# A fused linear attention and feed-forward kernel: the opening plan written anew, with batch 0's keys and values in the row layout of the later batches and w_out loaded in halves

## The chip, the cores and the metric

The kernel runs on one core of one Trainium2 chip. The metric is the device time of one execution in microseconds (us). The kernel before takes 250.07 us, the median of 3 runs (249.78 to 250.11).

## The reference

`q`, `k`, `v` have the shape 8 batches, 8 heads, 576 positions, 64 values, in fp32. The weights `w1`, `w2` are 512x1024, `w3` is 1024x1024, `w_out` 1024x512. Attention is linear, with ReLU features that are scaled by the cosine and the sine of the position:

```python
q_p = phi(q, cos_w, sin_w)          # [relu(x)*cos, relu(x)*sin], 128 features
k_p = phi(k, cos_w, sin_w)
kv = np.einsum('bhsf,bhsd->bhfd', k_p, v)
z = np.sum(k_p, axis=2)
num = np.einsum('bhsf,bhfd->bhsd', q_p, kv)
den = np.einsum('bhsf,bhf->bhs', q_p, z)[..., None] + 1e-06
attn = num / den                    # then heads are joined: x is 4608 x 512
out = ((x @ w1) * (x @ w2)) @ w3 @ w_out
```

## The kernel before

Attention works batch by batch, in five chunks of positions (four of 128 rows, one of 64). The feed-forward part works on nine tiles of 512 tokens. `w3 @ w_out` is multiplied once on the chip into `w34`, so that a tile needs only the products with `w1`, `w2` and `w34`.

The order of all work is a hand-written list, `PLAN`, whose steps are issued one after the other. Every engine runs its own instructions strictly in the order in which the steps issue them. The steps that matter here, with a batch `b` and a chunk `c`:

- `l b t h`, `lg`, `lt`: half `h` of tensor `t` of batch `b` is loaded by a DMA that POOL issues (`lg` and `lt` first wait for a result that is named in the code). `l0 ...`: the same for parts of batch 0. `w12 i c n`: `n` column blocks of 128 of `w1` (i=0) or `w2` (i=1). `w3 p`, `wo p`: pieces of `w3` and `w_out`. All these convert fp32 to bf16 on the way. Batch 0's keys alone are loaded by SP, in fp32.
- `k b c`, `q b c`: the features of keys and queries. VectorE (DVE) makes the cosine half (L502), ScalarE (ACT) the sine half (L505); a third number `n` gives the first `n` heads of the sine half to ScalarE and the rest to VectorE (L508).
- `v b c E`: the values are copied beside a column of ones, on engine E (V, A or G).
- `kv b` (L548), `kv0` (L746): the matmuls of keys and values. `kvs0`: their copies out of PSUM.
- `qt`, `qh`: a chunk of query features is transposed on TensorE (PE, L566 and L559) and copied out by the engine named. `qd` does the same by a DMA transpose that SP issues.
- `n b c` (L580): the numerators and denominators. `d b c` (L589 to L591): the division. `xt` (PE, L618) or `xd` (DMA): the transposes of the result into the tile `xT`.
- `t3 j`: VectorE transposes block `j` of 128 rows of `w3` (L464). `w j l n` (L480): `n` of the eight matmuls that make block `j` of `w34`; ScalarE copies it out (L483). Block `j` needs the rows of `w3` of that block in all four partition groups, and all of `w_out`.
- `f t`: the next step of tile `t`. A tile's steps are the products with `w1` and `w2` (L662), in two halves of 256 tokens for the first four column blocks of the tiles 0 and 1 and then one column block at a time; ScalarE copies the `w1` product (L686, L700) and VectorE multiplies it with the `w2` product (L688, L705). Tile 0 takes 16 steps of these. Then come 8 steps of output matmuls (L710). PSUM tiles of these products come from one pool of four buffers, used in turn.
- `idle n`: `n` matmuls on zeros, whose results nobody reads.

POOL has eight lanes for its loads: a load is issued when the load that was issued eight before it has landed. Both kernels have this through the framework. Before the first `f 0`, the plan is one long line; afterwards each line begins with one step of PE's main work.

In the layout of the batches 0 and 7 ("whole"), partition p holds positions 4p to 4p+3 of the first 512, and the last 64 positions are a chunk of their own, loaded by a separate DMA in pieces of 64 values. In the row layout of the batches 1 to 6, partitions 0 to 63 hold five positions each of the first 320, and partitions 64 to 127 four each of the last 256.

Of the kernel before, what the change touches and what calls it, by code (L numbers as in the profile page):

```python
# [10 lines left out]
FP32 = mybir.dt.float32  # L11
BF16 = mybir.dt.bfloat16
# [4 lines left out]
P = 128  # L17
H, S, D = 8, 576, 64
# [8 lines left out]
l0 q02; k 0 4; k 0 0; idle 10; l0 v4; v 0 0 A; w12 1 0 2; k 0 2; l0 q22; lg 1 q 0; l0 q4; lg 1 q 1; w12 0 0 2; w12 1 4 2; w12 0 2 2; v 0 4 V; v 0 1 V; v 0 2 A; k 0 3; w12 1 6 2; idle 3; w12 1 2 2; q 0 1; w12 0 4 2; w3 3; k 0 1; w3 1; qt 0 1 V; q 0 0 4; w12 0 6 2; wo 1; qc 0 3; v 0 3 A; wo 0; kv0; q 0 2; kvs0 1 A; kvs0 0 A; w3 0; wo 3; w3 2; qh 0 0 V; wo 2; qs 0 3; n 0 1; qt 0 2 A; w3 4; d 0 1; w3 5; qt 0 3 A; q 0 4; n0; w3 6; n 0 2; d 0 0; idle 3; d 0 2; xt 0 1 V; open; w3 7; xt 0 0 A; q 1 2; q 1 0; lg 1 k 0; n 0 3; qt 0 4 V; lg 1 k 1; lg 1 v 0; lt 1 v 1; xt 0 2 A; q 1 3; q 1 1; l 2 k 0  # L27
f 0
f 0; d 0 3
f 0; l 2 v 0  # L30
f 0; xt 0 3 V; qt 1 2 V; n 0 4; d 0 4
f 0
f 0; clear 1
f 0
f 0
f 0; xt 0 4 V
f 0
f 0; qt 1 0 V; lg 2 q 0; q 1 4; qt 1 3 A
f 0; qt 1 1 V
f 0  # L40
f 0; l 2 k 1; t3 0
f 0
f 0; t3 1; qt 1 4 A
w 0 0 4
w 0 4 4; l 2 q 1
w 1 0 4
w 1 4 4; t3 2; t3 3; t3 4
w 2 0 4
w 2 4 4; l 2 v 1; v 1 4 G
w 3 0 4; v 1 3 G; t3 5; v 1 1 G  # L50
w 3 4 4
w 4 0 4; k 1 2; l 3 q 0; t3 6
w 4 4 4; k 1 1; t3 7; k 1 4
w 5 0 4
w 5 4 4; k 1 0
w 6 0 4; v 1 2 V
w 6 4 4; v 1 0 V; k 1 3
w 7 0 4; kv 1
w 7 4 4; v 2 3 G; n 1 4; v 2 0 G
f 0; d 1 4  # L60
f 0; n 1 0; xd 1 4; d 1 0
f 0; q 2 1; v 2 4 G; lt 3 v 0; q 2 0
f 0; n 1 1; d 1 1; k 2 2
f 0; q 2 3
f 0; lg 3 q 1; v 2 1 G; l 3 v 1; q 2 4; k 2 0
f 0; n 1 2; d 1 2
f 0; xt 1 1 V; lt 3 k 0
f 1; k 2 3; xd 1 0; n 1 3; d 1 3; xt 1 2 V
f 1; qd 2 1
f 1; v 2 2 V  # L70
f 1; k 2 4; k 2 1
f 1
f 1; kv 2; l 3 k 1
f 1; qd 2 0; q 2 2; qd 2 2
# [237 lines left out]
def kernel(  # L312
# [53 lines left out]

    def load(b, name, part=None):
# [22 lines left out]
    def load_first(eng, t, src, c0=0, n=4):  # L390
        rows = src[0, :, 0:512, :].rearrange("h (p j) d -> p h j d", j=4)
        eng.dma_start(out=t[:, :, c0:c0 + n, :].rearrange("p h j d -> p h (j d)"),  # L392
                      in_=rows[:, :, c0:c0 + n, :].rearrange("p h j d -> p h (j d)"))

    def load_first4(eng, t, src):
        eng.dma_start(out=t[0:64, :, 4, :], in_=src[0, :, 512:S, :].rearrange("h p d -> p h d"))  # L396

    def load_w3(piece):

        half, a = divmod(piece, 4)  # L400
        nc.gpsimd.dma_start(out=w3b[ts(a, 32), ts(half, 4), :].rearrange("p g (c j) -> p (g c) j", c=4),
                            in_=moe_w3[ts(half, 512), ts(a, 256)].rearrange("(r i) j -> i r j", i=32))

    def load_wout(a):

        nc.gpsimd.dma_start(out=woutb[ts(a, 32), :, :],
                            in_=moe_w_out[ts(a, 256), :].rearrange("(l j) m -> j l m", j=32))

    def load_w12(c0, n):
        nc.gpsimd.dma_start(out=w1b[:, :, ds(c0, n)], in_=w1v[:, :, ds(c0, n)])  # L410
        nc.gpsimd.dma_start(out=w2b[:, :, ds(c0, n)], in_=w2v[:, :, ds(c0, n)])
# [7 lines left out]
    def load_first_parts(what):  # L419

        name, n = what[0], int(what[1])
        t, src = raw[0, name], {"v": v, "q": q}[name]
        if n == 4:
            load_first4(nc.gpsimd, t, src)
        else:
            load_first(nc.gpsimd, t, src, n, int(what[2]))
# [9 lines left out]
    def clear_rows(i):  # L436

        if i < NVA:
            nc.vector.memset(va_bufs[i][:, :, :, D:D + 1], 1.0)
            nc.vector.memset(va_bufs[i][64:128, 4, :, 0:D], 0.0)  # L440
        for fp in kp_bufs[i:i + 1] + qp_bufs[i:i + 1]:
            nc.vector.memset(fp[64:128, 4, :, :], 0.0)

    clear_rows(0)
# [13 lines left out]
    make_identity(nc, identb[:])  # L458


    def w3_tr(jp):

        w3T = sm.tile([P, 8, 128], BF16, name="w3T", bufs=NT3)
        nc.vector.transpose(out=w3T[:].rearrange("p l (c i) -> p l c i", c=4),  # L464
                            in_=w3b[:, jp, :].rearrange("p (c l j) -> p l c j", c=4, l=8))
        w3Ts[jp] = w3T

    def w3_dma(jp):
        w3Ts[jp] = sm.tile([P, 8, 128], BF16, name="w3T", bufs=NT3)
        nc.sync.dma_start_transpose(out=w3Ts[jp][:], in_=w3b[:, jp, :])  # L470
        transposed[0] = w3Ts[jp][:, 0, 0:1]
# [25 lines left out]
    def features(b, dst, src, c, n=H, cos=True, sin=True):  # L497

        R = ROWS[c]
        at = NCH + c if b in WHOLE else c  # L500
# [10 lines left out]
    def prep_k(b, c, n=H, **kw):  # L511
        features(b, att_of(b)["kp"], raw[b, "k"], c, n, **kw)

    def prep_q(b, c, n=H, **kw):
        features(b, att_of(b)["qp"], raw[b, "q"], c, n, **kw)

    def prep_v(b, c, copy=None):
        R = ROWS[c]
        (copy or nc.gpsimd.tensor_copy)(out=att_of(b)["va"][:R, c, :, 0:D], in_=raw[b, "v"][:R, :, c, :])  # L519
# [35 lines left out]
    def q_tr_halves(b, c, on):  # L555
        for half in range(2):
            pst = ps_tr.tile([P, 8, 128], BF16, name="pst")
            for i in range(4):
                nc.tensor.transpose(pst[:, i, :], att[b]["qp"][:, c, 4 * half + i, :], identb[:])  # L559
            on(out=att[b]["qpT"][:, ts(half, 4), ds(columns_of(b, c), 128)], in_=pst[:, 0:4, :])  # L560
# [178 lines left out]
    def kv_first():  # L739

        kp, va = att_of(0)["kp"], att_of(0)["va"]
        att[0]["kvs"] = sm.tile([P, H, D + 1], BF16, name="kvs", bufs=2)
        halves = att[0]["halves"] = (kva[:, :], pnum()[:, 0, :])
        for c in range(NCH):
            for h in range(H):
                nc.tensor.matmul(halves[h // 4][:, ds((h % 4) * 65, 65)], lhsT=kp[:, c, h, :],  # L746
                                 rhs=va[:, c, h, 0:D + 1], start=(c == 0 and h % 4 == 0),
                                 stop=(c == NCH - 1 and h % 4 == 3))
# [39 lines left out]
    def store_behind_transposes():  # L788
# [7 lines left out]
        "l": load, "lg": gated, "lt": behind_transposes, "l0": load_first_parts, "gx": behind_first_x,  # L796
# [44 lines left out]
```

## Time and profile before

| | us |
|---|---|
| median of 3 runs | 250.07 |
| the profiled execution, whole | 249.93 |
| its span, first to last instruction | 248.0 |
| what lies around the span | 1.93 |
| PE busy | 238.7 |
| VectorE busy | 141.4 |
| ScalarE busy | 126.7 |
| POOL busy | 85.0 |

PE is busy for 96% of the span. Its granted clock shows as full speed in all 40 slices. The profile's chain of work that ended last goes back through PE for 87% of the span and through DMA for 8%. Times in the text are counted from the start of the span. The landing of a load is the start of its issue on POOL plus the time to landing that the view of DMA issues gives. The sizes of that view are those in which the data land, in KB of 1024 bytes.

### The profile page before, as it was taken

To read this page: it belongs to the slowest core of one execution; us is meant where nothing else is said; L and a number is where in the kernel's file an instruction comes from. 1 tells how busy PE (TensorE), PEld (TensorE's weight loads), DVE (VectorE), ACT (ScalarE), POOL (GpSimd) and SP (SyncE) were. 2 spreads that over 40 slices of the span, in tenths; PEclk is the share of its full clock that TensorE was granted. 3 is DMA by queue.
4 is the path that set the end of the run, shared out by engine and by line. 5 is a ranking of instruction groups with operands and counts; after the bars stand their busy time and mean duration, and the time that the engine had idled before them with its cause. 6 is when DMAs were issued, how large, how long until landed. Compare 5 with 4: busy or idle time off the path is not lost.

```text
span 248.0 us, 4883 instructions
## 1 busy us (share of the span) xinstructions
PE 238.7 (96%) x1827; PEld 129.8 (52%) x1855; DVE 141.4 (57%) x342; ACT 126.7 (51%) x217; POOL 85.0 (34%) x162
## 2 busy tenths in 40 slices
PE   8969999999999999999999999999999999999994
PEld 3468754455974644445554545455444644444443
DVE  6498668768758545828685462577546607512420
ACT  2689243658566642765467334767643332323332
POOL 7664354534602042305310506207000100397800
PEclk9999999999999999999999999999999999999999
DMA  7999999999996989999999999999876431389933
GB/s 193 181 193 194 200 200 197 198 199 173 170 181 99 166 139 173 148 202 131 151 145 123 165 158 121 202 164 176 183 98 121 98 69 21 70 268 341 293 132 127
DMA packets 87223, 40.69 MB, mean 164 GB/s; under 512 B 51744, under 2 KB 84768, under 8 KB 87200
## 3 DMA queue, kind: packets, MB, share of 16 engines
q0 software_dynamic: 40144, 27.20, 69.6%
q1 hardware_dynamic: 47056, 13.18, 33.5%
q8 instruction: 14, 0.23, 0.4%
q14 instruction: 9, 0.07, 0.1%
HBM read 38.80 MB, written 9.44 MB: 194 GB/s over the span
## 4 chain that ended last, share of the span: by engine, by line
PE 87%; DMA 8%; POOL 2%; issue 1%; DVE 1%; ACT 0%; POOLq 0%; DVEq 0%
PE ffnps L662 49%; PE ffnps L710 24%; PE ffnps L480 5%; DMA w2b<-in_moe_w_dram 4%; PE pnum L580 4%; DMA qs<-in_q_dram 4%; PE pnum L548 4%; PE pst L566 1%; PE ffnps L727 1%; POOL vs L392 0%; POOL qs L392 0%; POOL w2b L770 0%; POOL vs L396 0%; PE pst L618 0%; DVE abT L705 0%
## 5 line engine op out<-in xcount | busy, mean ns | idle before, releaser
L705 DVE TENSOR_TENSOR abT<-asb,ffnps 128x512 bf16<-128x512 bf16 x64 | 43.7, 685 | 59.6 <-PE ffnps L662 56.7
L662 PE MATMUL ffnps<-xT,w2b 128*128 128x512 bf16 (+2 forms) x347 | 75.3, 340 | 0.9 <-DMA w2b<-in_moe_w_dram 0.3
L662 PE MATMUL ffnps<-xT,w1b 128*128 128x512 bf16 (+2 forms) x341 | 74.6, 339 | 0.5
L700 ACT CAST asb<-ffnps 128x512 bf16<-128x512 f32 x64 | 37.4, 584 | 53.7 <-PE ffnps L662 42.8
L710 PE MATMUL ffnps<-w34b,abT 128*128 128x512 bf16 x271 | 63.8, 379 | 0.5
L662 PEld LDWEIGHTS <-w2b 128*128 128x128 bf16 x352 | 31.5, 98 | 28.6 <-issue 0.5
L662 PEld LDWEIGHTS <-w1b 128*128 128x128 bf16 x352 | 31.7, 98 | 28.0
L710 PEld LDWEIGHTS <-abT 128*128 128x128 bf16 x280 | 26.1, 98 | 28.3
L505 ACT ACTIVATE kp<-kf,sinv 128x512 bf16<-128x512 bf16 (+3 forms) x40 | 28.0, 718 | 7.1 <-DMA kf<-in_k_dram 7.1
L505 ACT ACTIVATE qp<-qs,sinv 128x512 bf16<-128x512 bf16 (+2 forms) x40 | 28.0, 714 | 4.0 <-DMA qs<-in_q_dram 4.0
L591 DVE TENSOR_TENSOR xblk<-pnum,den 128x512 bf16<-128x512 f32 (+1 forms) x39 | 26.9, 691 | 2.5 <-DMA xT<-xblk 1.3
L417 POOL COPY seen<-asb 128x1 bf16<-128x1 bf16 x13 | 2.5, 194 | 54.6 <-ACT asb L700 54.6
L580 PEld LDWEIGHTS <-qpT 128*128 128x128 bf16 x320 | 15.3, 98 | 9.8 <-issue 0.9
L502 DVE TENSOR_SCALAR kp<-kf,cosv 128x512 bf16<-128x512 bf16 (+3 forms) x40 | 15.4, 404 | 7.3 <-DMA kf<-in_k_dram 7.2
L716 ACT COPY early<-ffnps 128x512 f32<-128x512 f32 x19 | 11.0, 581 | 15.8 <-PE ffnps L710 15.7
L580 PE MATMUL pnum<-kvs,qpT 128*128 128x65 bf16 x312 | 16.4, 194 | 1.4 <-DVE xblk L591 0.5
L716 ACT COPY osb<-ffnps 128x512 f32<-128x512 f32 x16 | 9.3, 584 | 14.8 <-PE ffnps L710 13.4
L519 POOL COPY va<-vs 128x512 bf16<-128x512 bf16 (+1 forms) x17 | 10.7, 648 | 17.5 <-DMA vs<-in_v_dram 17.5
L502 DVE TENSOR_SCALAR qp<-qs,cosv 128x512 bf16<-128x512 bf16 (+1 forms) x40 | 14.8, 389 | 1.9 <-DMA qs<-in_q_dram 1.9
L480 PE MATMUL ffnps<-early,w3T 128*128 128x512 bf16 x62 | 13.9, 379 | 0.1
L417 POOL COPY seen<-xT 128x1 bf16<-128x1 bf16 x8 | 1.6, 196 | 34.4 <-DMA xT<-xblk 34.4
L453 PE MATMUL unread<-zeros 128*128 128x512 bf16 x42 | 11.6, 441 | 1.2 <-DVE zeros L434 1.2
(86 smaller groups left out, 197.6 us busy)
## 6 DMA issues: line engine op xcount, KB each, us to landing
out_dram<-osb POOLq DMA_DIRECT2D x10, 256.0 KB, 4.5
qs<-in_q_dram POOLq DMA_DIRECT2D x8, 256.0 KB, 8.5
early<-in_moe_w_dram POOLq DMA_DIRECT2D x8, 256.0 KB, 10.3
qs<-in_q_dram POOLq DMA_DIRECT2D x6, 320.0 KB, 8.3
kf<-in_k_dram POOLq DMA_DIRECT2D x6, 320.0 KB, 8.0
vs<-in_v_dram POOLq DMA_DIRECT2D x6, 320.0 KB, 7.5
kf<-in_k_dram POOLq DMA_DIRECT2D x6, 256.0 KB, 6.8
vs<-in_v_dram POOLq DMA_DIRECT2D x6, 256.0 KB, 7.7
```

Of the source, the lines that this page charges most:

```text
L453: nc.tensor.matmul(unread[:, :], lhsT=zeros[:, 0:128], rhs=zeros[:], start=True, stop=True)
L480: nc.tensor.matmul(acc[:, :], lhsT=w3T[:, lc, :], rhs=woutb[:, lc, :], start=(lc == 0), stop=(lc == 7))
L502: nc.vector.tensor_scalar(out=dst[:R, c, :, 0:D], in0=src[:R, :, c, :], scalar1=0.0, scalar2=cosv[:R, at:at + 1], op0=ALU.max, op1=ALU.mult)
L505: nc.scalar.activation(out=dst[:R, c, 0:n, D:F], in_=src[:R, 0:n, c, :], func=ACTF.Relu, scale=sinv[:R, at:at + 1], bias=0.0)
L519: (copy or nc.gpsimd.tensor_copy)(out=att_of(b)["va"][:R, c, :, 0:D], in_=raw[b, "v"][:R, :, c, :])
L580: nc.tensor.matmul(nt[:, h // 4, ds((h % 4) * 65, 65)], lhsT=qpT[:, h, ds(at, 128)], rhs=kvs[:, h, :], start=True, stop=True)
L591: nc.vector.tensor_tensor(out=xblk[rows], in0=n4[:, :, :, 0:D], in1=den[rows].unsqueeze(3).to_broadcast([R, 2, 4, D]), op=ALU.mult)
L662: nc.tensor.matmul(out, lhsT=w[:, kc, ts(jc, 128)], rhs=x[:, kc, tok], start=(kc == 0), stop=(kc == 3))
L700: nc.scalar.copy(out=asb[:], in_=aT[:, :])
L705: nc.vector.tensor_mul(out=abT[:, jc, :], in0=asb[:], in1=bT[:, :])
L710: nc.tensor.matmul(ops[:, :], lhsT=abT[:, jc, ts(ms, 128)], rhs=w34b[:, jc, :], start=(jc == 0), stop=(jc == 7))
L716: nc.scalar.copy(out=osb[:, ms % 2, :], in_=ops[:, :])
```

## The change

The opening line of `PLAN` and the lines up to the second third of tile 1 are replaced. The functions that load batch 0, `w3` and `w_out` take other pieces.

- Keys and values of batch 0 are loaded in the row layout: one DMA for the partitions 0 to 63 and one for 64 to 127. Queries of batch 0 stay in the whole layout.
- `w3` comes in 16 pieces of 128 KB (two row blocks of one partition group) instead of 8 of 256 KB. `w_out` comes in 8 halves of 128 KB instead of 4 pieces of 256 KB.
- Batch 1's queries are loaded behind most of `w3` instead of ahead of `w1`. The features and transposes of batch 1's queries lie among the `w` steps or behind them, instead of among the products of tile 0.
- `kv0` goes chunk by chunk. A chunk whose values have not been copied is multiplied as 64 columns straight from the loaded values and one column from a new constant of ones (16 matmuls instead of 8).
- The first steps of `f 0` start after two chunks of batch 0; `kv 1` lies after `w 7`, not in the middle of it; steps of `f 1` are mixed with the last steps of `f 0`.
- The chunks `x 1 4`, `1 0` and `1 2` are transposed on PE and `1 1` and `1 3` by DMA. Before, `1 1` and `1 2` went through PE and `1 4`, `1 0` and `1 3` through DMA.

```diff
-l0 q02; k 0 4; k 0 0; idle 10; l0 v4; v 0 0 A; w12 1 0 2; k 0 2; l0 q22; lg 1 q 0; l0 q4; lg 1 q 1; w12 0 0 2; w12 1 4 2; w12 0 2 2; v 0 4 V; v 0 1 V; v 0 2 A; k 0 3; w12 1 6 2; idle 3; w12 1 2 2; q 0 1; w12 0 4 2; w3 3; k 0 1; w3 1; qt 0 1 V; q 0 0 4; w12 0 6 2; wo 1; qc 0 3; v 0 3 A; wo 0; kv0; q 0 2; kvs0 1 A; kvs0 0 A; w3 0; wo 3; w3 2; qh 0 0 V; wo 2; qs 0 3; n 0 1; qt 0 2 A; w3 4; d 0 1; w3 5; qt 0 3 A; q 0 4; n0; w3 6; n 0 2; d 0 0; idle 3; d 0 2; xt 0 1 V; open; w3 7; xt 0 0 A; q 1 2; q 1 0; lg 1 k 0; n 0 3; qt 0 4 V; lg 1 k 1; lg 1 v 0; lt 1 v 1; xt 0 2 A; q 1 3; q 1 1; l 2 k 0
+q0 0 2; k 0 0 4; idle 1; k 0 2; q0 4 1; q0 2 2; k 0 1; w12 1 2 2; w12 1 0 2; v 0 3 A; v 0 4 V; idle 1; idle 1; w12 0 0 2; w12 0 4 2; v 0 2 V; w12 0 2 2; k 0 3; k 0 4; idle 2; w12 0 6 2; idle 1; kv0 2 0; kv0 0 1; w12 1 6 2; idle 1; wo 3 0 4; w12 1 4 2; q 0 0 4; kv0 1 1; kv0 3 1; qh 0 0 A V; idle 3; q 0 1 4; kv0 4 2; kvs0 0 A; kvs0 1 V; qt 0 1 A; n0; idle 1; idle 2; d 0 0; idle 2; wo 0 4 4; n 0 1; w3 2 0 2; idle 1; q 0 2; wo 1 0 4; w3 3 2 2; xt 0 0 A; wo 1 4 4; qt 0 2 A; d 0 1; idle 1; idle 2; wo 0 0 4; q 0 3; wo 2 0 4; xt 0 1 V; w3 3 0 2; w3 0 0 2; open; wo 3 4 4; w3 1 0 2; w3 2 2 2; wo 2 4 4; w3 1 2 2; w3 2 4 2; w3 0 2 2; w3 3 4 2; l 1 q 0; w3 1 4 2; w3 0 4 2; q 0 4; l 1 q 1
+f 0; w3 1 6 2; w3 2 6 2; w3 3 6 2; w3 0 6 2; n 0 2; l 1 k 0; d 0 2
+f 0; l 1 k 1; qt 0 3 V
+f 0; l 1 v 0; l 1 v 1; xt 0 2 V; n 0 3
...
+f 0; xt 0 4 V; t3 0
 f 0
+f 0; lg 2 q 0; t3 1
 f 0
+f 0; t3 2; l 2 v 0
 f 0
+f 0
 w 0 0 4
+w 0 4 4; t3 3
 w 1 0 4
+w 1 4 4
 w 2 0 4
+w 2 4 4; clear 1; t3 4; q 1 0
+w 3 0 4
+w 3 4 4; l 2 k 1; q 1 4 2; l 2 q 1; v 1 4 G; t3 5
+w 4 0 4; q 1 2; q 1 1; t3 6
+w 4 4 4; qt 1 0 A; q 1 3 2; l 2 v 1
+w 5 0 4; qt 1 4 A
+w 5 4 4; v 1 1 G; t3 7
+w 6 0 4; k 1 4; v 1 3 G; k 1 2; k 1 1 4; k 1 0 4; qt 1 1 V; k 1 3 4
+w 6 4 4; l 3 q 0; v 2 4 G
+w 7 0 4; qt 1 3 A; v 1 0 V; v 1 2 V
+w 7 4 4; kv 1
+f 0; n 1 4
+f 0; d 1 4; qt 1 2 V; n 1 0; d 1 0
+f 0; xt 1 4 V
+f 0; n 1 1; lt 3 v 0; d 1 1; q 2 1
+f 0; xt 1 0 V; v 2 3 G; l 3 v 1; k 2 0
+f 0; q 2 3; v 2 2 G; n 1 2; v 2 1 G; lg 3 q 1; d 1 2
+f 1
+f 1; q 2 4; q 2 0; k 2 2; v 2 0 G; xd 1 1
+f 0; n 1 3; lt 3 k 0; d 1 3
+f 1; qd 2 1; k 2 3 2
+f 0; v 3 3 G
+f 1; q 2 2; xt 1 2 V; k 2 4; second; k 2 1
...
+    def load_rows(eng, t, rows, half):
+        j, span = (5, slice(0, 320)) if half == 0 else (4, slice(320, S))
+        eng.dma_start(out=t[ts(half, 64), :, 0:j, :].rearrange("p h j d -> p h (j d)"),
+                      in_=rows[:, span, :].rearrange("h (p j) d -> p h (j d)", j=j))
...
+    def load_w3(a, g0, n):
+        nc.gpsimd.dma_start(out=w3b[ts(a, 32), ds(g0, n), :].rearrange("p g (c j) -> p (g c) j", c=4),
+                            in_=moe_w3[ds(128 * g0, 128 * n), ts(a, 256)].rearrange("(r i) j -> i r j", i=32))
+    def load_wout(a, l0=0, n=8):
+        rows = moe_w_out[ts(a, 256), :].rearrange("(l j) m -> j l m", j=32)
+        nc.gpsimd.dma_start(out=woutb[ts(a, 32), ds(l0, n), :], in_=rows[:, ds(l0, n), :])
...
+    for eng, t, src in ((nc.sync, k0, k), (nc.gpsimd, raw[0, "v"], v)):
+        load_rows(eng, t, src[0], 0)
+        load_rows(eng, t, src[0], 1)
...
+            if c in copied:
+                nc.tensor.matmul(out, lhsT=kp[:, c, h, :], rhs=va[:, c, h, 0:D + 1],
+                                 start=(first and h % 4 == 0), stop=(last and h % 4 == 3))
+                continue
+            nc.tensor.matmul(out[:, 0:D], lhsT=kp[:, c, h, :], rhs=v0[:, h, c, :],
+                             start=(first and h % 4 == 0), stop=False)
+            nc.tensor.matmul(out[:, D:D + 1], lhsT=kp[:, c, h, :], rhs=oneb[:],
+                             start=False, stop=(last and h % 4 == 3))
```

160 lines of the change are left out of this document (53 added, 107 removed).

## The prediction

> **What bounds the kernel now.** I read the page's 40 slices first. They show TensorE (PE), the DMA share, and the GB/s that the loads bring, each slice 6.2 us:
>
> ```profile
> PE   8969999999999999999999999999999999999994
> DMA  7999999999996989999999999999876431389933
> GB/s 193 181 193 194 200 200 197 198 199 173 170 181 99 166 139 173 148 202 131 151 145 123 165 158 121 202 164 176 183 98 121 98 69 21 70 268 341 293 132 127
> ```
>
> PE is full from about 25 us to the end. DMA is full too up to about 56 us, at 193 to 200 GB/s. So two things are full at once in the front, and the last wait there tells which counts. That is in the chain of waits (start, length, what):
>
> ```profile
> 5.83 9.19 DMA qs<-in_q_dram
> ...
> 15.30 9.93 DMA w2b<-in_moe_w_dram
> ...
> 25.28 4.80 PE ffnps L662 x57
> ...
> 38.88 7.13 PE ffnps L480 x33
> ...
> 51.84 1.29 PE pnum L548 x40
> ```
>
> Up to 25.28 the end hangs on loads, behind it on PE alone. An earlier start of PE is worth something only as far as PE then finds its data. Two meetings with the loads are in the timelines of VectorE (DVE) and PE, and in the DMA issues of single moments:
>
> ```profile
> 37.42 1.24 DVE L464 STREAM_TRANSPOSE w3T<-early 128x1024 bf16<-128x1024 bf16 x1
> ...
> 38.72 2.55 PE L480 MATMUL ffnps<-early,w3T 128*128 128x512 bf16 x11
> ...
> 51.68 1.44 PE L548 MATMUL pnum<-va,kp 128*128 128x65 bf16 x40
> ```
>
> ```profile
> early<-in_moe_w_dram POOLq DMA_DIRECT2D x1, 256.0 KB, 10.0
> vs<-in_v_dram POOLq DMA_DIRECT2D x1, 256.0 KB, 10.4
> ```
>
> The first load is the `w3` piece issued at 27.30; it lands at 37.3, the first `t3` starts at 37.42, and `w 0` at 38.72. The second is the last half of batch 1's values, issued at 39.50; it lands at 49.9, and `kv 1` starts at 51.68. PE meets both without idling.
>
> **The loads.** POOL's loads land in order of issue, so I add up KB in that order, with the 1152 KB of batch 0's keys in front, and take the landing that the kernel before has at the same sum. Before: 2880 KB 16.9 us, 3136 18.1, 3392 20.5, 3648 21.2, 4416 25.2, 4672 27.1, 5696 32.1, 5952 33.3, 6208 34.7, 6464 35.9, 7232 40.1, 7488 41.3, 8000 43.9, 9152 49.9. After, with the new order: `w1` 0 and 1 (3072) 17.8; `w1` 2 and 3 (3584) 21.1; `w2` 4 and 5 (4480) 25.7; the `w3` rows of blocks 0 and 1 (5888) 33.05; the last half of `w_out` (6144) 34.4; blocks 2 and 3 (6528) 36.3; batch 1's queries (7488) 41.3; all of `w3` (8000) 43.9; batch 1's values (9152) 49.9. From 8000 KB on the two orders have moved the same bytes. This is the main point: `w3` for the first `t3` comes 4.25 us sooner, batch 1's keys and values not at all.
>
> Two corrections. The row layout does away with two pieces of 64-value rows (128 KB of keys, 64 KB of values). The 64 KB piece landed 0.5 us behind the load before it (11.28, 11.78), where 197 GB/s make 0.33; at the same rate both pieces cost some 0.5 us more than their bytes. Over 4 to 11 us the one-us windows show 158, 196, 179, 186, 183, 197 and 184 GB/s, 90 kB short of 196, which is also 0.5 us. Some of that is the start itself. Ends 0 and 0.5, taken 0.3. The Trainium skill ("DMA: Bandwidth & Descriptors", Rules for kernel authors) says that two transfers to disjoint partition halves serialize and bring nothing; by that rule alone this term is 0 and the forecast below would be 0.3 us later.
>
> The other correction is 24 pieces of 128 KB (131 kB). At 199 GB/s one is due every 0.66 us. POOL's rows give 0.58 us for 256 descriptors (`wo`) and 0.65 for 512 (`w3`), and a half piece has 128 or 256, so 0.5 to 0.6 us: taken as hidden. If it is not, see the third rival.
>
> **PE up to `w`.** Attention of batch 0: values land at 10.1; ScalarE then copies one chunk (0.52 a piece) and makes two key features (0.62 each), to 11.9; the queries are there at 11.8 and half a sine (0.40) ends at 12.3; PE transposes (0.45), idles on purpose (0.65) and ends `kv0` at 13.8 (15.6 before). `kvs0` to 14.3, `n0` 0.4, two divisions of 1.1 each with a feature of 0.3 between them, and `xt 0 1`: `f 0` can start at 17.5, and `w1` lands at 17.8. Before, it started at 21.26. The gaps of PE stay under the 1.4 us that PE had ahead of 13.57 with its clock granted in full, so I charge no clock.
>
> Steps 1 to 8 of tile 0 are 7.1 us of products (16 x 0.224 and 4 x 0.875). With three `n` (0.26), two `qt` (0.45), two `xt` (0.22) and 0.2 of waiting for `w1` at 20.8 they end at 27.3. Steps 9 to 16 are 0.864 each; step 16 would start at 33.6.
>
> It does not. `t3 0` stands in VectorE's queue behind the product of step 10, and its data land at 33.05, so VectorE stands still with the multiplication of step 12 behind `t3 0`. PE has four PSUM buffers in turn: step 16 needs the one of step 12. That is free at 33.05 + 0.05 + 1.2 (`t3`) + 0.6 (multiplication) = 34.95, and step 16 ends at 35.8: PE waits 1.3 us and gives back that much of its early start. By the same count nothing waits behind it: `t3 1` to `t3 7` end at 36.1, 37.9, 39.7, 41.3, 43.5, 45.3 and 47.2, each over 1 us ahead of its `w`.
>
> **`w` to `kv 1`.** Before: 51.68 - 38.72 = 12.96 us, which is 60 matmuls of 0.216. After: all 64 (13.82) and four `qt 1` (1.8), moved here from among tile 0: 15.6 us. 35.8 + 15.6 = 51.4, less the 0.3 of the loads: `kv 1` at 51.1. Its own data are nearly as late: values at 49.6, copied by 50.7 to 51.1 for the chunks in their order. So of 3.5 us at the first `f 0` 0.6 are left.
>
> **Behind `kv 1`.** The `w` matmuls that lay there are gone (4 x 0.216 = -0.86), `qt 1 2` (+0.45) and a third `xt` (+0.22) are new: -0.19. The order of `f 0`, `n 1` and `f 1` leaves 1.6 us or more from one `n 1` to the next, and the rows before show 1.5 to 1.6 (54.04 to the end of the division, 55.59): nothing, at most 0.3. Batch 2's loads have the same sums.
>
> **Sum.** (51.1 - 51.68) - 0.19 = -0.77 us. The profiled execution took 249.93 (248.0 and 1.93 around it; the median of the runs is 0.14 higher): 249.93 - 0.77 = 249.2. About 0.2%, or 0.5 us, is what a measurement can tell here from no change, so faster is below 249.57. With the unknown terms (0 to 0.5 for the small rows, 0 to 0.3 behind `kv 1`) this case spans 248.7 to 249.6.
>
> **The rivals.**
>
> *The stop at `t3 0` costs nothing* (chance 0.1). If PE passes step 16 in time, `w 0` starts at 34.4, and `kv 1` waits for its values alone: copies of the first two chunks at 50.3. (50.3 - 51.68) - 0.19 = -1.6: 248.3. This is the floor, since the sum of bytes ahead of the values is unchanged. Against it stands the strict order of VectorE.
>
> *`kv 1` waits for its inputs* (0.18). POOL copies `v 1 4`, issues a load, and copies `v 1 1` and `v 1 3`: 48.6 + 4 x 0.7 = 51.4, and `kv 1` needs `v 1 3` 1.0 us after its start. ScalarE has 8.2 us of work in the 7.5 us ahead of `kv 1` (four `w34` copies, the features of the queries and keys, three `qt` copies). Half a microsecond late in either and all is taken back: about 249.9, no change.
>
> *The small pieces starve the DMA: slower* (0.14). Decisive is whether a piece costs POOL over 0.66 us. If it keeps 0.78, as `w12` issues take (0.74 to 0.79), 24 pieces are 24 x 0.12 = 2.9 us late; `t3 0`, behind eleven of them, 1.3 us. Then values land at 52.5 and `kv 1` starts at about 53.3: +1.6 - 0.19 = +1.4, 251.4. For it: eight lanes hold only 1 MB now, which is 5.3 us of moving, where 2 MB took 10.5 before. Against it: a load of 320 KB that met an empty queue (98.40) landed in 4.9 us, 1.6 of them moving, so a lane turns around in some 3.3 + 0.3 + 0.7 = 4.3 us, under 5.3. The Trainium skill ("DMA: Bandwidth & Descriptors", Bandwidth) speaks against the change here: it asks for DMAs of at least 1 MiB. By the fixed 2.0 us for each DMA that the same page gives (Anatomy of one DMA), eight in flight would still cover it: as an estimate, no delay.
>
> *Tile 1 waits for `x 1 1`: slower* (0.08). Its DMA transpose is issued at about 58.5 and PE asks for it at 65.3. Before, the like took 4.9 us. Should it queue behind 1.4 MB of loads (7 us) and the rest follow, PE idles about 1 us: 250.3.
>
> **How the numbers follow.** Forecast 0.50, rivals 0.10, 0.18, 0.14 and 0.08. Faster is nearly all of the forecast (0.46) and the first rival: 0.56. The same is most of the second and the edge of the forecast: 0.20. Slower is the rest, 0.24. The range goes from the first rival (248.3, less 0.1) to 250.7, which takes in the second and fourth and leaves out most of the third.
>
> **What would show it.** First `f 0` at 17.5 to 18.5 us (L662). VectorE idle ahead of the first L464, ended by a `w3` load near 33; PE idle about 1 us near 34, put down to the L705 multiplication. First L480 at 35 to 36, `kv 1` (L548) at 50.8 to 51.5. The loads of batch 1's values land at 49.4 to 49.9. Wrong would be: GB/s under 190 between 25 and 44 us (the third rival); the idle time ahead of L548 itself, put down to values or keys (the second); idle time of PE near 65 (the fourth); or a first `f 0` later than 19, since 1.1 us is all that the stop at `t3 0` covers.

## The result and the profile after

The changed kernel takes 251.39 us (median of 13 runs, 250.54 to 253.43), the kernel before on the same chip 250.11 us (13 runs, 249.13 to 251.19). The ratio is 1.0067, with a 95% interval of 1.0040 to 1.0094: slower, where 249.2 and faster was forecast, and outside the range of 248.2 to 250.7. A run more than 1.5% above the fastest of its kernel is left out of the ratios (two runs of e8 and one of e11 below), which are estimated from all the other runs and not from the medians. The profiled execution took 251.17 us, with a span of 249.1.

The page of the kernel after, the same three rows of its 40 slices as were shown of before:

```profile
PE   8779999999999999999999999999999999999994
DMA  6999999999999779998999998999755431279953
GB/s 129 213 194 197 199 181 194 199 199 193 152 175 161 141 121 181 158 159 139 160 161 133 191 157 97 179 163 191 177 108 102 101 71 22 45 210 331 307 209 126
```

The first slice has 129 GB/s, where it had 193. That is 6.2 us of missing bytes right at the start: 64 GB/s x 6.2 us = 0.4 MB. In the next eight slices both move 181 to 213 GB/s. The chain of waits (start, length, what) names who waits for them:

```profile
1.55 9.94 DMA kf<-in_k_dram
```

The chain now begins with batch 0's keys (`kf`), which were nowhere in it before. The DMA issues of the first 3 us (KB, then us to landing), first of after, then of before:

```profile
kf<-in_k_dram SPq DMA_DIRECT2D x1, 640.0 KB, 6.1
kf<-in_k_dram SPq DMA_DIRECT2D x1, 512.0 KB, 9.9
```

```profile
kf<-in_k_dram SPq DMA_DIRECT2D x1, 1024.0 KB, 6.4
```

The same 1152 KB are complete at 1.55 + 9.94 = 11.5 us instead of 7.75 (there the last 128 KB are issued at 1.25 and need 6.5). What follows from that is in the timelines of VectorE and PE, first of before, then of after:

```profile
7.73 1.70 DVE L502 TENSOR_SCALAR kp<-kf,cosv 64x512 bf16<-64x512 f32 x3 [1.23 <-DMA kf<-in_k_dram]
...
13.57 0.61 PE L566 MATMUL pst<-identb,qp 128*128 128x128 bf16 x8 [1.41 <-DVE qp L502]
```

```profile
11.59 0.49 DVE L488 TENSOR_SCALAR kp<-kf,cosv 128x512 bf16<-128x512 f32 x1 [4.60 <-DMA kf<-in_k_dram]
...
33.68 1.25 DVE L457 STREAM_TRANSPOSE w3T<-early 128x1024 bf16<-128x1024 bf16 x1 [0.54 <-DMA early<-in_moe_w_dram]
```

```profile
13.71 0.29 PE L738 MATMUL kva<-va,kp 128*128 128x65 bf16 x4 [3.00 <-DVE va L509]
...
20.84 0.39 PE L652 MATMUL ffnps<-xT,w1b 128*128 128x128 bf16 x4
...
37.49 8.80 PE L467 MATMUL ffnps<-early,w3T 128*128 128x512 bf16 x40
...
53.09 1.44 PE L538 MATMUL pnum<-va,kp 128*128 128x65 bf16 x40
```

The bracket is the idle time ahead of the instruction and what ended it. VectorE stands still for 4.60 us until keys land (1.23 before); PE then idles 3.00 us, where it idled 1.41 before (its releaser, the copy of values, stands behind the late key features in VectorE's queue). The first `f 0` starts at 20.84 (forecast 17.5, before 21.26), `w 0` at 37.49 (35.8, before 38.72), and `kv 1` at 53.09 (51.1, before 51.68). From 20 us to `kv 1` PE never idles.

The rest is arithmetic. `kv 1` is 53.09 - 51.68 = 1.41 us later than before, and `kv 4` only 117.68 - 116.68 = 1.00. Of the difference, 0.22 is a wait of PE in the profile of before, for which after has no counterpart:

```profile
101.49 1.02 PE L662 MATMUL ffnps<-xT,w2b 128*128 128x512 bf16 x4 [0.22 <-DVE abT L705]
```

From `kv 4` to the end of the span nothing differs by more than 0.1: before takes 131.3 us (116.68 to 248.0) and after 131.4 (117.68 to 249.1). Around the span lie 2.07 us instead of 1.93. So the profiled execution is 1.24 us longer (251.17 against 249.93). The whole question is why the front lost 1.4 us where it should have won 0.6.

### The profile page after: what moved, and what is told of

It reads as the page before. It is cut to its first block, busy times and chain, and to the rows that moved or that the text cites. A ratio compares the mean times of both kernels' runs of the same rounds, so it can differ in the third digit from the quotient of the medians.

```text
span 249.1 us, 4973 instructions
## 1 busy us (share of the span) xinstructions
PE 241.3 (97%) x1878; PEld 130.7 (52%) x1878; DVE 143.1 (57%) x353; ACT 124.4 (50%) x215; POOL 91.9 (37%) x174
## 4 chain that ended last, share of the span: by engine, by line
PE 92%; DMA 4%; ACT 2%; DVE 0%; SPq 0%; issue 0%; ACTq 0%
PE ffnps L652 50%; PE ffnps L700 24%; PE ffnps L467 6%; PE pnum L570 4%; DMA kf<-in_k_dram 4%; PE pnum L538 4%; PE pst L556 1%; ACT kp L491 1%; PE unread L447 1%; PE pst L608 1%; PE ffnps L717 1%; SPq L370 0%; PE pst L549 0%; ACT va L509 0%; DVE kvs L543 0%
## 5 line engine op out<-in xcount | busy, mean ns | idle before, releaser
L652 PE MATMUL ffnps<-xT,w1b 128*128 128x512 bf16 (+2 forms) x352 | 76.0, 341 | 0.1
L700 PE MATMUL ffnps<-w34b,abT 128*128 128x512 bf16 x280 | 65.2, 379 | 0.0
L491 ACT ACTIVATE kp<-kf,sinv 128x512 bf16<-128x512 bf16 (+7 forms) x40 | 26.1, 682 | 9.4 <-DMA kf<-in_k_dram 9.4
L491 ACT ACTIVATE qp<-qs,sinv 128x512 bf16<-128x512 bf16 (+4 forms) x40 | 26.9, 692 | 3.2 <-DMA qs<-in_q_dram 1.9
L488 DVE TENSOR_SCALAR kp<-kf,cosv 128x512 bf16<-128x512 bf16 (+3 forms) x40 | 14.6, 385 | 7.3 <-DMA kf<-in_k_dram 7.3
L509 POOL COPY va<-vs 128x512 bf16<-128x512 bf16 (+1 forms) x18 | 11.3, 638 | 14.9 <-DMA vs<-in_v_dram 8.3
L467 PE MATMUL ffnps<-early,w3T 128*128 128x512 bf16 x64 | 14.6, 380 | 0.0
L447 PE MATMUL unread<-zeros 128*128 128x512 bf16 x46 | 13.1, 437 | 1.2 <-DVE zeros L425 1.2
```

Of the source, the lines that this page charges most:

```text
L447: nc.tensor.matmul(unread[:, :], lhsT=zeros[:, 0:128], rhs=zeros[:], start=True, stop=True)
L467: nc.tensor.matmul(acc[:, :], lhsT=w3T[:, lc, :], rhs=woutb[:, lc, :], start=(lc == 0), stop=(lc == 7))
L488: nc.vector.tensor_scalar(out=dst[:R, c, :, 0:D], in0=src[:R, :, c, :], scalar1=0.0, scalar2=cosv[:R, at:at + 1], op0=ALU.max, op1=ALU.mult)
L491: nc.scalar.activation(out=dst[:R, c, 0:n, D:F], in_=src[:R, 0:n, c, :], func=ACTF.Relu, scale=sinv[:R, at:at + 1], bias=0.0)
L652: nc.tensor.matmul(out, lhsT=w[:, kc, ts(jc, 128)], rhs=x[:, kc, tok], start=(kc == 0), stop=(kc == 3))
L700: nc.tensor.matmul(ops[:, :], lhsT=abT[:, jc, ts(ms, 128)], rhs=w34b[:, jc, :], start=(jc == 0), stop=(jc == 7))
```

## The experiments

All ratios are against the kernel before on the same chip, with 95% intervals. "Theory P" says that a DMA that reaches only 64 partitions moves the fp32 keys at a limited rate; its rival "S" says that the keys merely share the DMA with the values and queries behind them.

### The whole layout put back in the changed kernel (e1_whole_kv)

```diff
     for eng, t, src in ((nc.sync, k0, k), (nc.gpsimd, raw[0, "v"], v)):
-        load_rows(eng, t, src[0], 0)
-        load_rows(eng, t, src[0], 1)
+        eng.dma_start(out=t[:, :, 0:4, :].rearrange("p h j d -> p h (j d)"),
+                      in_=src[0, :, 0:512, :].rearrange("h (p j) d -> p h (j d)", j=4))
+        eng.dma_start(out=t[0:64, :, 4, :], in_=src[0, :, 512:S, :].rearrange("h p d -> p h d"))
...
-        features(att_of(b)["kp"], raw[b, "k"], c, NCH + c if b == 7 else c, n, **kw)
+        features(att_of(b)["kp"], raw[b, "k"], c, NCH + c if b in WHOLE else c, n, **kw)
```

> The changed kernel with one part undone: keys and values of batch 0 are loaded in the whole layout again (512 positions over 128 partitions, the last 64 by a DMA of their own). Theory P (a DMA that reaches only 64 partitions writes fp32 at no more than about 220 GB/s, so the keys land at 11.5 instead of 7.7): keys land at 7.5 to 7.8, kv0 starts near 10.8 with no idle time of PE ahead of it, first f 0 at 17.5 to 18.5. Behind that the stop at t3 0 then shows (0.5 to 1.3 us of PE idle near 34 to 35), kv 1 near 51.7 to 52, and the whole is 249.8 to 250.4: about the kernel before. Theory S (the values' DMA takes the engines away from the keys, whatever the layout): keys land later than 9 again, f 0 at 19.5 or later, whole above 250.6.

249.44 us (12 runs, 248.89 to 251.43) against 250.32; ratio 0.9979 (0.9957 to 1.0001). This one part of the change makes the difference between a loss of 1.28 us and a gain of 0.88 (each against the median of its own runs of before): 2.2 us. The one-us window from 4 to 5 us, first of before, then of after, then of this kernel (the columns: the window and its sum; the busy shares and counts of PE, its weight loads, VectorE, ScalarE and POOL; granted clock, DMA share, GB/s):

```profile
4.00:5.00 1.00, 1.00 (x3) 0.30 (x2) 0.89 (x4) 0.00 (x0) 1.00 (x2) 1.00 1.09 387
```

```profile
4.00:5.00 1.00, 1.00 (x3) 0.30 (x2) 0.90 (x4) 0.00 (x0) 1.00 (x3) 1.00 1.16 221
```

```profile
4.00:5.00 1.00, 1.00 (x3) 0.30 (x2) 0.93 (x3) 0.00 (x0) 1.00 (x2) 1.00 1.08 383
```

From 5 to 6 us it is 190 in after against 331 here. The keys need 5.7 and 6.0 us from issue to landing instead of 6.1 and 9.9. With them in time, the forecast's own steps up to `t3 0` come out one by one. First `f 0` is at 17.51 (forecast 17.5). That line of PE's timeline, then `t3 0` in VectorE's, and then what PE does beside it:

```profile
17.51 0.39 PE L653 MATMUL ffnps<-xT,w1b 128*128 128x128 bf16 x4
```

```profile
32.69 1.25 DVE L458 STREAM_TRANSPOSE w3T<-early 128x1024 bf16<-128x1024 bf16 x1 [2.58 <-DMA early<-in_moe_w_dram]
33.85 0.65 DVE L696 TENSOR_TENSOR abT<-asb,ffnps 128x512 bf16<-128x512 bf16 x1
```

```profile
33.59 1.03 PE L653 MATMUL ffnps<-xT,w2b 128*128 128x512 bf16 x4
34.45 1.89 PE L468 MATMUL ffnps<-early,w3T 128*128 128x512 bf16 x8
```

`t3 0` is at 32.69 (forecast 32.75) and VectorE idles ahead of it, as forecast. But PE does not stop. Step 16 of tile 0 starts at 33.59, before the multiplication of step 12 begins (33.85). At that moment four results are in PSUM: the `w2` products of steps 12 and 14, which wait for VectorE, the `w1` product of step 15, and that of step 16 itself. The `w1` products of steps 11 and 13 have been copied out by ScalarE, so two buffers came free out of turn. The four are not used strictly in turn, as the description of the kernel has it; one that is free is given out. `w 0` starts at 34.45 instead of the forecast 35.8.

Then two small waits take that back, in PE's timeline:

```profile
44.20 1.04 PE L468 MATMUL ffnps<-early,w3T 128*128 128x512 bf16 x4 [0.51 <-DVE w3T L458]
...
51.36 1.28 PE L539 MATMUL pnum<-va,kp 128*128 128x65 bf16 x32 [0.21 <-DVE va L510]
```

`t3 5` stands in VectorE's queue behind features of batch 1's queries, which landed at 42.0 (34.28 + 7.69 in the chain of waits), and `kv 1` meets its values: they land at 50.49 (42.27 + 8.22) instead of the forecast 49.6.

### Row layout alone, in the kernel before (e2_rows_in_before)

```diff
-    load_first(nc.sync, k0, k)
-    load_first4(nc.sync, k0, k)
-    load_first(nc.gpsimd, raw[0, "v"], v)
+    load_rows0(nc.sync, k0, k, 0)
+    load_rows0(nc.sync, k0, k, 1)
+    load_rows0(nc.gpsimd, raw[0, "v"], v, 0)
...
```

(`load_rows0` is `load_rows` of the changed kernel; the second half of the values is loaded where the plan had `l0 v4`, and the key features use the positions of the row layout.)

> The kernel before with one part of the change alone: keys and values of batch 0 in the row layout, half by half (the second half of the values is issued where their last 64 positions were). Theory P: keys land at 11 to 11.6, everything of batch 0 slips by 3 to 3.8 us, first f 0 near 24 to 25, and since PE is busy without a gap from there on nearly all of it is paid: 252.3 to 253.6. Rival (the front waits for the order of the loads, not for the keys): keys land by 8.5, f 0 by 22, whole within 0.2% of the kernel before.

252.96 us (6 runs) against 250.32; ratio 1.0104 (1.0078 to 1.0129). The layout by itself costs 2.6 us in the old order, as theory P expected, so the new order isn't needed for the loss. The keys land at 1.5 + 8.8 = 10.3, somewhat sooner than expected, and the first `f 0` starts at 24.78. PE's timeline shows a second effect, which is part of the 2.6:

```profile
15.90 1.03 PE L574 MATMUL pst<-identb,qp 128*128 128x128 bf16 x8 [3.71 <-ACT qp L513]
16.73 0.43 PE L754 MATMUL kva<-va,kp 128*128 128x65 bf16 x4
```

After 3.71 us of idling the same matmuls take longer: 1.03 us for eight transposes, which take 0.61 in the timeline of the kernel above, and 0.43 instead of the 0.29 of after's `kv0`. The granted clock of the span was 0.986 to 0.993 in every run here; in the changed kernel, with 3.00 us of idling, it was 0.991 to 0.993 in 4 of 13, and in the runs of the kernel before that stand beside the experiments in 10 of 67.

### The keys with nothing beside them (e3_keys_alone)

```diff
-    for eng, t, src in ((nc.sync, k0, k), (nc.gpsimd, raw[0, "v"], v)):
-        load_rows(eng, t, src[0], 0)
-        load_rows(eng, t, src[0], 1)
+    load_rows(nc.sync, k0, k[0], 0)
+    load_rows(nc.sync, k0, k[0], 1)
...
     make_identity(nc, identb[:])
+    gate(k0[:, 0, 0, 0:1])
+    load_rows(nc.gpsimd, raw[0, "v"], v[0], 0)
+    load_rows(nc.gpsimd, raw[0, "v"], v[0], 1)
```

> The changed kernel with the loads of batch 0's values (and all of POOL's loads behind them) held until the keys have landed, so that the keys move alone. Its whole time means nothing; the keys' landing and the GB/s of the first 10 us count. Theory P: 200 to 220 GB/s between 3 and 7 us, keys at 8.3 to 9.3. Theory S: 350 to 390 GB/s, keys at 6 to 7.

The windows, with no other load on the way:

```profile
3.00:4.00 1.00, 1.00 (x4) 0.33 (x3) 0.87 (x5) 0.00 (x0) 0.00 (x0) 1.00 0.95 276
4.00:5.00 1.00, 1.00 (x5) 0.35 (x4) 0.83 (x6) 0.00 (x0) 0.00 (x0) 1.00 1.16 212
5.00:6.00 1.00, 1.00 (x6) 0.48 (x5) 0.86 (x6) 0.00 (x0) 0.00 (x0) 1.00 1.12 189
...
7.00:8.00 1.00, 1.00 (x6) 0.43 (x5) 0.00 (x0) 0.00 (x0) 0.00 (x0) 1.00 1.13 190
```

Alone, from 4 us on, the keys get 189 to 222 GB/s (222 from 6 to 7). That is about what all loads together move in the changed kernel from 4 to 7 us (221, 190, 210), so the limit is the keys' own: theory P, and not S. The us from 3 to 4 runs faster than P said, at 276 (269 in after, against 326 in e1 and 359 in before); no run shows why the limit sets in only then. The keys land at 9.2 instead of 11.5; sharing that limited rate with the values adds the other 2.3 us. (The whole time, 256.34 us, means nothing, since every other load waits.)

### The two halves on two queues (e9_two_queues)

```diff
-        load_rows(eng, t, src[0], 1)
+        load_rows(nc.scalar if eng is nc.sync else eng, t, src[0], 1)
```

> The changed kernel with the second half of batch 0's keys issued by ScalarE's queue instead of behind the first half on SP's, so that both halves of the partitions are written at the same time. Theory P1 (the limit belongs to the half of the partitions, not to the queue): 300 GB/s or more between 3 and 6 us, both halves land at 7 to 8.5, first f 0 by 18.8, whole 249.2 to 250.2. Theory P2 (two DMAs side by side share one limit, as the Trainium skill's SBUF page has it, which measured 6% for such a pair): 200 to 230 GB/s as before, keys at 10 or later, first f 0 later than 20, whole above 250.6.

```profile
5.00:6.00 1.00, 1.00 (x6) 0.44 (x5) 0.84 (x6) 0.00 (x0) 1.00 (x2) 1.00 1.13 220
```

There are still 199, 220 and 206 GB/s in the windows from 4 to 7 us. Both halves are issued at 0.74 us, but they do not move side by side. The queues of the first 6 us (packets, MB, share; q10 is ScalarE's, q1 is SP's):

```profile
q10 hardware_dynamic: 528, 0.52, 49.4%
q1 hardware_dynamic: 162, 0.21, 17.3%
```

ScalarE's half of 512 KB (0.52 MB) is through while SP's has moved 0.21 of its 0.66 MB; they land at 6.3 and 9.6. So a second queue brings nothing, as P2 said (which had the keys at 10 or later). Whether two halves that did move together would add up, this run can't tell. The first `f 0` starts at 21.53. 252.22 us (4 runs) against 250.61; ratio 1.0097 (1.0060 to 1.0134): no better than the changed kernel. The Trainium skill ("SBUF — State Buffer", "Can I just issue two DMAs to hit both halves?") has two concurrent DMAs on partitions 0 and 64 at only 6% over one, since they serialize; this trace agrees (199 to 220 GB/s, one half after the other).

### Two DMAs in the whole layout (e11_whole_in_two)

```diff
...
+        for half in range(2 if eng is nc.sync else 1):
+            ps, span = (ts(half, 64), ts(half, 256)) if eng is nc.sync else (slice(0, 128), slice(0, 512))
+            eng.dma_start(out=t[ps, :, 0:4, :].rearrange("p h j d -> p h (j d)"),
+                          in_=src[0, :, span, :].rearrange("h (p j) d -> p h (j d)", j=4))
...
```

This is e1 with one difference (the lines stand in place of e1's DMA of the first 512 positions): the keys' first 512 positions go to the same places in two DMAs of 64 partitions instead of one of 128.

> The kernel with the whole layout (e1), whose 512 positions of batch 0's keys are loaded by two DMAs of 64 partitions, one behind the other, instead of one of 128. Rows, their length (1024 bytes) and their order in memory are those of e1. Theory N (what counts is that one DMA reaches only 64 partitions): 200 to 230 GB/s between 4 and 7 us, keys at 9.5 to 11.5, first f 0 at 19.5 to 21, whole 250.5 to 252. Rival (the row layout's five positions to a row, or its access pattern, is slow): 320 GB/s or more, keys by 8, first f 0 by 18.3, whole as e1 (249.4).

```profile
4.00:5.00 1.00, 1.00 (x6) 0.49 (x5) 0.93 (x3) 0.00 (x0) 1.00 (x2) 1.00 1.19 194
```

383 and 331 GB/s become 194 and (from 5 to 6 us) 197, with rows of the same 1 KB (four positions of 64 fp32 values). 251.90 us (8 runs) against 250.17; ratio 1.0061 (1.0035 to 1.0086), the loss of the changed kernel again; the first `f 0` starts at 21.39. The values are in the whole layout here, so the keys alone make the loss. Nor is it that there are two DMAs: in e3 the first half has landed at 0.7 + 6.0 = 6.7, and from 7 to 8 us the second, alone on its way, still gets 190 GB/s. It is the number of partitions that a DMA reaches, and not the layout, that costs.

### The row layout with keys converted to bf16 (e5_rows_bf16_keys)

```diff
-    k0 = raw[0, "k"] = kf[:].rearrange("p (h c d) -> p h c d", h=H, c=NCH)
+    k0 = raw[0, "k"] = kf[:, 0:1280].bitcast(BF16).rearrange("p (h c d) -> p h c d", h=H, c=NCH)
...
-    for eng, t, src in ((nc.sync, k0, k), (nc.gpsimd, raw[0, "v"], v)):
+    for eng, t, src in ((nc.gpsimd, k0, k), (nc.gpsimd, raw[0, "v"], v)):
```

> The changed kernel, row layout kept, but batch 0's keys are loaded by POOL and converted to bf16 on the way like every later batch's, ahead of the values on the same queue. Theory P (64 partitions take no more than about 220 GB/s, which hurts fp32 keys alone, since converted loads write half the bytes and run at 195 to 200 GB/s anyway): keys land at 6.5 to 7.5, values at 9.5 to 10.3, first f 0 at 17.3 to 18.3, whole 249.0 to 249.9. Rival (the halves are slow by themselves, through their 512 descriptors or their order, in any type): keys later than 9, first f 0 later than 19.5, whole above 250.6.

The second half of the keys in the DMA issues at the start (KB as landed):

```profile
kf<-in_k_dram POOLq DMA_DIRECT2D x1, 256.0 KB, 5.1
```

Loads that convert move about 195 GB/s anyway (189 to 195 from 4 to 7 us here, counted as landed), and half the partitions do not slow them: the two halves need 4.6 and 5.1 us, with half the bytes to write, instead of 6.1 and 9.9. `f 0` starts at 18.18, `kv 1` at 51.01, and the span is 247.6, close to e1. The median is 250.68 (12 runs, up to 253.41) against 250.61; ratio 1.0022 (0.9995 to 1.0049). So the mechanism is confirmed in the trace, but the time lies above the expected 249.0 to 249.9 and recovers only in part; the long runs, at a granted clock of 0.998 or more, stay unexplained here.

### PE's idle time filled (e4_gap_filled)

```diff
-    idle_mms(27)
+    idle_mms(41)
```

> The changed kernel with 41 instead of 27 matmuls on zeros at the start, which fill the 3.0 us in which PE stands idle ahead of kv0. Theory C (the wait of 3 us costs the TensorE clock in about half of the runs, 1 to 2 us each time): granted clock 1.000 in every run, whole 250.5 to 251.2 in all of them, median near 250.9. Rival (the scatter of the changed kernel has another cause): runs up to 253 remain, clock below 0.995 in some.

252.47 us (6 runs, 251.65 to 254.06) against 250.32; ratio 1.0088 (1.0057 to 1.0118). The granted clock is back at 0.997 to 1.000, and the time is not better, so the rival holds: the scatter has another cause too. The run doesn't price the clock, though. In its profile `kv 1` starts at 52.71, 0.38 us sooner than in the changed kernel, and the way from `kv 3` to `kv 4` takes 31.74 us instead of 31.05, with PE waiting 0.44 us at 111.18 for a DMA transpose of `x`. The changed kernel's own runs price it: the four with the clock below 0.995 take 252.95 us in the mean, the other nine 251.34. That is about 0.5 us of the 1.67 by which its mean lies above the kernel before; the larger part is there at full clock as well.

### Three attempts on what e1 leaves

Batch 1's queries behind its keys and values, with their features and transposes behind `kv 1` (e8_queries_behind_values):

```diff
-... w3 3 4 2; l 1 q 0; w3 1 4 2; w3 0 4 2; q 0 4; l 1 q 1
+... w3 3 4 2; w3 1 4 2; w3 0 4 2; q 0 4
-f 0; l 1 v 0; l 1 v 1; xt 0 2 V; n 0 3
+f 0; l 1 v 0; l 1 v 1; l 1 q 0; l 1 q 1; xt 0 2 V; n 0 3
...
+f 0; q 1 4; q 1 0
+f 0; qt 1 4 A; q 1 1; qt 1 0 V
+f 0; n 1 4; q 1 2
+f 0; d 1 4; n 1 0; q 1 3; qt 1 1 A; d 1 0; l 3 q 0; v 2 4 G
```

> The kernel with the whole layout (e1) and batch 1's queries loaded behind its keys and values, their features and transposes behind kv 1. Theory V (in e1 kv 1 waits for the values, which land at 50.5 since the queries' 576 KB are ahead of them): values land at 47 to 48, kv 1 starts at 48.3 to 49.2 right behind w 7, PE's waits of 0.5 us at w 5 and 0.2 us in kv 1 are gone, and the whole is 0.4 to 1.0 us below e1: 248.4 to 249.1. Rival (the queries are then late): PE idles ahead of qt 1 or f 1, and the whole is that of e1 (249.4) or above.

`kv 1` starts at 48.69, 2 us ahead of e1, as theory V said, but the span grows to 248.6 and the median is 250.84 against 250.61 (ratio 1.0021, 0.9996 to 1.0046). Of the 2 us, 1.8 are the four transposes of 0.45 that now lie behind `kv 1`: moved, not saved. And PE waits there:

```profile
62.09 0.42 PE L571 MATMUL pnum<-kvs,qpT 128*128 128x65 bf16 x8 [0.45 <-DVE xblk L582]
```

There is 0.34 at 55.23 of the same kind and 0.17 at 66.41 for a DMA transpose of `x`, together 0.96 us. From `kv 1` to `kv 2` e8 takes 22.13 us and e1 19.38: 2.75 more, which is 1.8 + 0.96. The gain is given back.

`w_out` in four pieces of 256 KB, as before, in e1 (e12_w_out_whole):

```diff
-wo 3 0 4; ... wo 0 4 4; ... wo 1 0 4; ... wo 1 4 4; ... wo 0 0 4; ... wo 2 0 4; ... wo 3 4 4; ... wo 2 4 4
+wo 3; ... wo 1; ... wo 0; ... wo 2
```

> The kernel with the whole layout (e1), w_out in 4 pieces of 256 KB instead of 8 halves. Theory H (POOL issues a small piece every 0.57 to 0.65 us without a pause, so the DMA queue runs nearly empty and loses 0.5 us near 30 to 33 us): the GB/s of these slices stay at 180 or more, batch 1's values land 0.2 to 0.6 us sooner than in e1 (50.5), kv 1 likewise; t3 0 gets its data 0.6 us later, which PE may just feel; whole 248.9 to 249.6. Rival (the dip has another cause): 150 to 175 GB/s somewhere in 29 to 34 us again, values at 50.3 to 50.7, whole as e1.

In e1 a stretch runs below the 190 to 200 GB/s of the loads; one window of e1, then of e12 (the next has 164 and 192 GB/s):

```profile
30.00:31.00 1.00, 1.00 (x7) 0.41 (x6) 0.10 (x1) 0.58 (x1) 0.87 (x3) 1.00 1.10 157
```

```profile
30.00:31.00 1.00, 1.00 (x7) 0.41 (x6) 0.31 (x2) 0.46 (x1) 0.58 (x1) 1.00 1.43 192
```

POOL, the fifth busy column, is at 0.9 with pieces of 128 KB and at 0.6 with 256: it issues back to back and the queue runs short. Without the dip the values are copied at 49.65 instead of 50.58, and `kv 1` starts at 50.38 without a wait, as theory H said. The time does not follow: 249.97 us (10 runs) against 250.17, ratio 1.0005 (0.9980 to 1.0031). In the profile this kernel is 0.84 us ahead of e1 at `kv 2` (69.27 against 70.11) and 0.24 behind at `kv 4` (116.04 against 115.80).

`t3 5` ahead of batch 1's query features, in e1 (e13_t3_ahead):

```diff
-w 2 4 4; clear 1; t3 4; q 1 0
+w 2 4 4; clear 1; t3 4; t3 5; q 1 0
-w 3 4 4; l 2 k 1; q 1 4 2; l 2 q 1; v 1 4 G; t3 5
+w 3 4 4; l 2 k 1; q 1 4 2; l 2 q 1; v 1 4 G
```

> The kernel with the whole layout (e1), t3 5 issued ahead of batch 1's first query features, so that it no longer waits for the queries' load behind them in VectorE's queue. Theory V (the values bind kv 1, not w 5): PE's wait of 0.5 us at w 5 goes, but kv 1 waits that much longer for the copy of the values (up to 51.2 to 51.4 for its second chunk), and the whole stays within 0.3 us of e1 (249.4). Rival (the wait at w 5 is what counts): kv 1 runs through from 50.2, whole 248.8 to 249.1.

The wait of `w 5` is gone (0.21 is left at `w 4`), and the values bind in its place, as theory V said, in PE's timeline:

```profile
51.53 1.28 PE L539 MATMUL pnum<-va,kp 128*128 128x65 bf16 x32 [0.18 <-DVE va L510]
...
101.29 1.02 PE L653 MATMUL ffnps<-xT,w1b 128*128 128x512 bf16 x4 [0.68 <-ACT asb L691]
```

250.64 us (12 runs) against 250.17; ratio 1.0011 (0.9987 to 1.0034), more than the 0.3 us above e1 that theory V allowed. The last line, with 0.42 us more at 102.73, shows a source of differences between runs far from the front: batch 4's queries landed late and held up VectorE's queue. The profile of before has 0.22 us there, those of after and e1 nothing.

So e1 is the best version seen, 0.9979 of before; its interval just touches 1, while the changed kernel's begins at 1.004.

## Why the prediction was wrong, step by step

**The loads (the step that failed).** "After, with the new order" put the keys' 1152 KB at the same landing as before, because it counted KB alone. They land at 11.5 instead of 7.75. A DMA that reaches 64 partitions moves fp32 keys at 189 to 222 GB/s from 4 us on (e3 and e9; 221 from 4 to 5 us in after), one of 128 partitions at 331 to 387 (e1 from 4 to 6 us, before from 3 to 5). All that the forecast hung on the keys moves with it: values and key features, the first `f 0` from 17.5 to 20.84, `w 0` to 37.49. The layout's price is 2.2 us by e1 and 2.6 by e2 (with the lower clock that its wait brings), and e11 shows that the partitions make it. No rival had it: all four began behind the first 17 us. Of the signs of being wrong, a first `f 0` later than 19 came true. The third rival's GB/s under 190 showed as well (181 in the slice from 31 to 37 us), and 251.39 is its 251.4; that is chance, since PE meets `kv 1` without a wait and the loss was made by 20.84.

The Trainium skill ("SBUF — State Buffer", Door 1: The DMA port swizzle) says this beforehand: partitions 0 to 63 reach 8 of the 16 ports, 196 GB/s at 1 MiB against 328 for 128 partitions. The trace agrees (189 to 222 against 331 to 387). The prediction had drawn on the neighbouring rule, that two halves "bring nothing", and read it as a price of nothing; by the one-us windows the price was about half the rate (221 GB/s instead of 387 from 4 to 5 us). That rule was also weighed against the wrong term, the 0.3 us for small rows. It would have been testable before: from 3 to 5 us the windows of before run at 359 and 387 GB/s, twice the 193 to 200 of the loads that convert, and they are the keys' alone. The prediction had this in hand: the row that it calls one-us windows from 4 to 11 us has slices of 1.5 us, so that it stands for 6.0 to 16.5 us, and the two slices just ahead, from 3.0 to 6.0, have 368 and 301 GB/s.

**The stop at `t3 0` (failed too, hidden by the first).** The 1.3 us rested on four buffers in turn (its sum, 33.05 + 0.05 + 1.2 + 0.6, is 34.90 and not 34.95, which changes nothing). e1 has PE pass step 16 without a wait, and `w 0` at 34.45 where the first rival said 34.4. In the changed kernel there is no stop either: 37.49 - 20.84 = 16.65 us from `f 0` to `w 0`, where the forecast without a stop needs 34.4 - 17.5 = 16.9.

**Batch 1's values (mis-sized).** Forecast 49.6; 50.49 in e1 and later in the changed kernel. The third rival was right in kind: the pieces of 128 KB leave the queue short for some us (157 and 164 GB/s in e1, 192 in both windows of e12). POOL issues one every 0.65 us at best (four from 29.68 to 32.27 in e1), which is just the rate that the DMA moves, so that a pause is not made up. It cost about 0.9 us of the values' copy, by e12, and not the 2.9 us that it was priced at. The second rival, `kv 1` waiting for its inputs, is there in e1 with 0.21 us of idle time.

**"I charge no clock" (failed).** PE idles 3.00 us ahead of `kv0` instead of under 1.4, and the granted clock falls below 0.995 in 4 of 13 runs (before: 10 of 67). e2, with 3.71 us, has it in all of its 6 runs and shows the slow matmuls. A window of e9, whose profiled run has the lower clock, shows it (the column ahead of the last two):

```profile
15.00:16.00 1.00, 1.00 (x11) 0.95 (x10) 0.00 (x0) 0.30 (x1) 1.00 (x3) 0.50 1.45 197
```

The clock there is 0.50 from 14.2 to 17.6 us, 3.4 us long, after PE had idled 3.17 us and worked for 1.2. The Trainium skill ("TensorE: Matmul & The Clock Gate", What's actually happening) has the clock at half after an idle window of about 3.4 us, in windows that run freely. The length of the slow stretch agrees, and a phase that differs from run to run would fit counts like 4 of 13; that the idle time has to fill a window does not agree, since 3.17 us were enough. The clock accounts for about 0.5 us of the mean loss (see e4), so it is a part of the result and not its main cause.

**What held.** The 15.6 us from `w 0` to `kv 1` (53.09 - 37.49 = 15.60). In e1, without the keys' delay, the first `f 0` (17.51 for 17.5) and `t3 0` (32.69 for 32.75). That e1's 249.44 lies so near to the forecast 249.2 is partly luck: the stop that didn't come (-1.3) and the late inputs ahead of `kv 1` nearly cancel. It is luck, too, that 1.41 at `kv 1` less the forecast 0.19 comes within 0.02 of the measured 1.24: between `kv 1` and `kv 4` 0.41 was gained, 0.22 of it by a wait of before, and 0.24 was lost behind it.

**What stays open.** Why the us from 3 to 4 still has 269 to 297 GB/s with loads to 64 partitions (e11 the most), before the limit shows, and whether two such loads would add up if they moved at the same time (in e9 they did not). And the spread of some versions: e4, e5, e8, e9 and e11 have single runs of 253 to 256 us. The profiles show one stretch that differs: from `kv 3` to `kv 4` e1 takes 31.04 us, before 31.43, e8 31.62, e4 31.74, e12 31.97 and e13 32.46, with waits of PE for late loads or transposes. That is where e12 loses what its front gains; what makes the loads late there was not tested.

## What to carry to other kernels

Before a layout is changed, count the partitions that each of its DMAs reaches: two transfers of 64 partitions in place of one of 128 nearly halved the rate of an unconverted load here (221 GB/s instead of 387), and its bytes said nothing of it. When bytes are summed against the landings of another kernel, the sum holds only for loads of the same shape and queue. A gain at the start of a chain is worth what the next full resource leaves of it: in e1, 3.75 us at the first `f 0` became 0.9 us at the end, and even that is hardly clear of the noise.

## What was not expected of the hardware

- An fp32 load to 64 partitions ran at 189 to 222 GB/s from 4 us on (e3), and a second one, issued at the same time on another queue for the other 64, moved behind the first and not beside it (e9). Loads that convert to bf16 ran at 189 to 195 GB/s, as landed, in the same halves (e5), about as fast as the 193 to 200 of the kernel before.
- While POOL issued pieces of 128 KB without a pause, the DMA fell to 157 and 164 GB/s for two us; with four pieces of 256 KB among them it kept 192 (e1, e12).
- Idle PE ahead of `kv0` cost granted clock (below 0.995) more often the longer it was in the profiled run: with 3.7 us in 6 of 6 runs (e2), with 3.0 to 3.2 us in 8 of 25 (after, e9, e11), with the 1.4 us of the kernel before in 10 of 67, with 0 to 0.9 us in 1 of 64 (e1, e4, e5, e8, e12, e13). In the profiled run of e9 the clock was at half for 3.4 us.
